# Delta-rule attention and MLP on one core: a new written-out order of the same operations

## The chip, the cores and the metric

The kernel runs on one core of a Trainium2 chip. The metric is the device time of one execution in microseconds (us), taken as the median of several runs. The engines are PE (TensorE, matrix products), DVE (VectorE), ACT (ScalarE), POOL (GpSimd) and SP (SyncE, which only issues transfers here). PEld in a profile is PE's weight loads.

## The reference

Four batches of eight heads run a recurrence over 768 tokens with a state of 48x48, and the 3072 rows of 384 that come out pass through an MLP with 2048 hidden units. Inputs and output are float32.

```python
def _attn_ref(q, k, v, beta):              # q, k, v: (4, 8, 768, 48)
    k_n = k / (np.linalg.norm(k, axis=-1, keepdims=True) + 1e-06)
    state = np.zeros((B, H, D, D), dtype=np.float32)
    for t in range(S):
        kt, vt, bt = (k_n[:, :, t].copy(), v[:, :, t].copy(), beta[:, :, t, None].copy())
        y[:, :, t] = np.einsum('bhd,bhde->bhe', q[:, :, t], state)
        v_old = np.einsum('bhde,bhd->bhe', state, kt)
        state = state + bt[:, :, :, None] * np.einsum('bhd,bhe->bhde', kt, vt - v_old)
    return y

def _moe_ref(x, w_in, w_out):              # x: (3072, 384), w_in: (384, 2048), w_out: (2048, 384)
    h = x @ w_in
    c = np.float32(np.sqrt(2.0 / np.pi))
    g = 0.5 * h * (1.0 + np.tanh(c * (h + 0.044715 * h * h * h)))
    return g @ w_out
```

## The kernel before

The tokens are cut into 12 chunks of 64. A chunk has two units (unit u belongs to chunk u // 2); a unit holds two of the four batches, one in each half of the 128 partitions, with eight heads along the free dimension. Data is bfloat16 on chip, products sum in float32 in PSUM, which has 8 banks.

The functions `load`, `norms`, `prep`, `chain` and `mlp` don't issue anything: each registers named operations with `A(engines, name, function, ...)`, together with what they read, write, allocate in PSUM and free. A name has the operation and, after the dot, its chunk or unit.

- `load(c)`: transfers of k, q and v in pieces (k3.10, q2.1, v5.01) into three raw buffers of each, taken in turn. `weights()` has four transfers from GpSimd's queue: w1.0 and w1.1 (halves of the first matrix), w2.0 and w2.1 (halves of the second). down00 to down11 read w2.0.
- `norms(c)`: sq, sum, pow, eps, nsq (or nsa on ACT), inv, ib: the norms of k and beta over their squares.
- `prep(u)`: kc, kb, qb cast and scale the tokens; T or turn (a transposing transfer) with kT turn them; GM, GQ, G2 and G form products of keys and queries (L528); ln, wpm, wpq and wp mask them (L532); X10 and X11 start an inverse (L562) and five steps refine it: A1 to A5 and B1 to B5 (L573, eight matmuls each) with rt1 to rt5 between them (L585). Each step's result goes from PSUM into a block-diagonal buffer, by one of three ways: bde (two copies of a half, L331), bdf (a copy of a half, then L337 over all partitions) or xi with two bdc (L331, L615). A step's J, C and rj are another way to its A and rt.
- `chain(c)`: the recurrence from chunk to chunk: vs, K (L645), R, Q, U (L668), Un, S (L680), Sn, O (L693), On, and X with xT or the transfer turnx. K, Q, S and O are 32 small matmuls each.
- `mlp(c)`: up0 to up15 (three matmuls each, L722), gelu0 to gelu3 (L726), down00 to down13 (four matmuls each, L733), Z0 and Z1 (L331) and the transfers out (L742, L745). up0 to up7 read w1.0, up8 to up15 w1.1.
- fill operations are products of zeros on PE in the first part.

What runs where and when is written out by hand in `ORDER`, one long text of some 1,700 words: a word is an operation's name, `:d`, `:a` or `:g` puts it on DVE, ACT or GpSimd in place of its first engine, `@n` gives its PSUM bank. Each engine works off its words in their order; `Flow.emit` puts the semaphore waits in front of an operation that needs what another engine or a transfer makes. So where an operation waits, all later words of its engine wait behind it. The place of a word relative to words of other engines means nothing for the time by itself.

Of the kernel before, what the change touches and what calls it, by code (L numbers as in the profile page):

```python
# [21 lines left out]
eps.0a betaN000 pad3:g k1.10 k1.01 kc.1 k2.00 nsq.0a inv.0a twob:d q0.1 k2.10 mlo1 pow.0b eps.0b:g q0.0:a nsq.0b:g sq.1:d v0.01:a betaA111
J1.1@3 ib.0a kb.0:g Tb.0@0 inv.0b ib.0b:g kb.1:g sum.1 kTc.0 fill4@1 betaA110 betaA101 pow.1 eps.1 nsq.1 k2.01 v0.11 inv.1 kTb.0 Tc.1@4
betaA100 ib.1:g Tb.1@2 kTb.1 kb.3:g GM.0@6 ln.0 ladj16 bdz0:g X11.0 kTc.1:a v0.10 qb.0:a GM.1@4 ln.1 X10.1:d fill45@2 fill16@1 kc.3 Tk.3@2
v0.00 fill42@0 two X10.0 Tq.0@1 X11.1 k2.11 pad2:g q1.0:a v1.10 wpm.0 A1.0@0 kTk.3:a GM.3@6 triln3 wpm.1 C1.1 sq.2 rj1.1 rt1.0 B1.0@0
# [24 lines left out]
turn.11 B4.7@1 G.9@4 wp.9 G2.9@6 ln.9 B4.6@0 up4.2@2 up5.2 up6.2 up7.2 bde40.6 up0.2@4 up8.2@6 up9.2 up10.2 up11.2 bde41.6 A5.6@0 bdc10.8:d  # L50
k8.01 xi4.7 bdc41.7 bdc40.7 kc.14 gelu1.2 up1.2 A5.7@1 up2.2 A2.8@2 up3.2 sum.7 rt5.6 rt5.7 B5.7@3 gelu2.2 sum.6 k8.10 X10.9 X11.9 A1.9@1
rt1.9 B5.6@0 up12.2@6 up13.2 up14.2 up15.2 B1.9@1 kc.13 gelu0.2 down00.2@4 bde51.7:d rt2.8 q6.0 kc.15 bde50.7 gelu3.2 q8.1 bde50.6:d K.3@2
R.3 bdf10.9 bdf11.9:d pow.6 bde51.6 G2.10@6 ln.10 B2.8@5 down01.2 pow.7 eps.6 U.3@2 v4.10 xi2.8:d bdc20.8:d bdc21.8 down02.2 v6.11 Q.3@0
# [8 lines left out]
On.4 kb.15:g A3.11@2 down00.3@4 A1.12@5 sq.8 B3.10@6 down12.3 v7.11 bde31.10 kb.14:g bde30.10 rt3.11 B3.11@0 bde31.11 out11.1 bde30.11
down01.3 down02.3 q10.0 sum.8 K.5@6 vs.5 rt1.12 B1.12@2 bde11.12 turnx.4 q8.0 A4.10@5 rt4.10 X11.13 A1.13@0 k9.00 rt1.13 bde10.12 down03.3
A4.11@5 rt4.11 Z0.3 B4.10@1 bdf40.10 turn.15 bdf41.10 down13.3 Z1.3 R.5 B4.11@0 bde41.11:d bde40.11 qb.19:g B1.13@2 up12.4@4 up13.4 bde11.13
A5.10@1 rt5.10 A2.12@3 up14.4 rt2.12 up8.4@6 B5.10@0 bde51.10:d pow.8 bde10.13 up15.4 gelu3.4 B2.12@1 bde21.12:d up9.4 A5.11@2 rt5.11 up10.4
up11.4 up0.4@4 B5.11@2 xi5.11:d up1.4 up2.4 bdc51.11:d bde50.10 A2.13@0 rt2.13 up3.4 bde20.12 gelu2.4 gelu0.4 A3.12@2 rt3.12 fill66@1
# [192 lines left out]
def bass_deltanet__then__act_gelu_tanh_kernel(  # L259
# [9 lines left out]
    B, H, S, D = q.shape  # L269
# [11 lines left out]
    A = F.add  # L281

    with nc.allow_non_contiguous_dma("strided loads"), nc.allow_low_precision("bf16 pipeline"):
# [185 lines left out]
        def prep(u):  # L469
# [26 lines left out]
            def kcopy(e, P, name, ys):  # L496
                return copy(e, kT[s][:, ys[0]:ys[-1] + 1, :, :].rearrange("p y g t -> p (y g t)"), P(name).bitcast(BF16)[:, 0:512 * len(ys)])
# [299 lines left out]
```

## Time and profile before

| | |
|---|---|
| median of 3 runs | 264.72 us (264.1, 264.72, 266.91) |
| the profiled execution | 265.58 us, span 263.8 us |
| instructions | 12,223 |
| PE busy | 244.8 us, 93% (5480 matmuls) |
| PEld busy | 190.2 us, 72% |
| DVE busy | 208.1 us, 79% |
| ACT busy | 186.5 us, 71% |
| POOL busy | 136.1 us, 52% |
| DMA | 31.86 MB, mean 121 GB/s |

The profile is of one execution. A row of a group gives the line, engine, operation and tile, the count, the busy time, the mean of one in ns, and the idle time of the engine before them with what ended it. "issue" stands for time in which an engine waited for nothing that the profile shows. The granted clock is the share of full speed that TensorE was given; where it is 0.50 a matmul takes twice as long. Rows of stretches give each engine's busy us with its count, then the granted clock, the DMA share and GB/s.

### The profile page before, as it was taken

The page shows a single profiled execution, that of the slowest core. Times are in us where ns is not written, and L with a number is a line of the kernel's source. Part 1 is how long each engine was busy: PE and PEld are TensorE (multiplying, and loading weights), DVE is VectorE, ACT ScalarE, POOL GpSimd, SP SyncE. Part 2 cuts the span into 40 slices and gives each one's busy share as a digit, 9 for nine tenths or more (in the row PEclk, how much of TensorE's full clock was granted, in tenths as well). Part 3 has the DMA queues.
Part 4 walks back from the last instruction along what each step waited for, and adds up shares of the span by engine and source line. Part 5 has one row for each costly group of instructions (what it writes and reads, how often), then busy time and mean ns, then how long its engine had stood idle before and what let it go on. Part 6 is the DMA issues. An engine that isn't in the chain of part 4 may idle for free.

```text
span 263.8 us, 12223 instructions
## 1 busy us (share of the span) xinstructions
PE 244.8 (93%) x5480; PEld 190.2 (72%) x5480; DVE 208.1 (79%) x355; ACT 186.5 (71%) x297; POOL 136.1 (52%) x197
## 2 busy tenths in 40 slices
PE   5697978699999999999999999998999999999994
PEld 1265657567787876887887988786968878878672
DVE  5788989668888898897898977999899989865000
ACT  0759878448788986988985887785855846776452
POOL 6379794679683888549266644684334120130000
PEclk9659999779999999999999999999999999999999
DMA  5999999969599984997936979631747824002122
GB/s 103 182 192 133 213 211 130 191 113 161 107 184 159 118 173 95 165 180 150 164 72 110 148 145 125 99 78 32 156 80 133 156 46 94 12 6 62 30 62 60
DMA packets 118356, 31.86 MB, mean 121 GB/s; under 512 B 112416, under 2 KB 117536, under 8 KB 118304
## 3 DMA queue, kind: packets, MB, share of 16 engines
q1 hardware_dynamic: 103408, 25.01, 56.4%
q0 software_dynamic: 2880, 3.15, 8.1%
q10 hardware_dynamic: 12016, 2.92, 5.8%
q8 instruction: 43, 0.70, 1.1%
q14 instruction: 9, 0.07, 0.1%
HBM read 20.64 MB, written 4.72 MB: 96 GB/s over the span
## 4 chain that ended last, share of the span: by engine, by line
PE 75%; DVE 7%; ACT 6%; DMA 4%; issue 3%; POOL 2%; SPq 1%; ACTq 0%; POOLq 0%
PE ps L733 23%; PE ps L722 20%; PE ps L573 18%; PE ps L528 4%; DMA kT<-tok 3%; PE ps L645 2%; ACT bd L331 2%; DMA qraw<-in_q_dram 2%; PE ps L668 2%; PE ps L693 2%; DVE rt L585 1%; PE ps L680 1%; PE ps L393 1%; DVE rl L585 1%; PE ps L493 1%
## 5 line engine op out<-in xcount | busy, mean ns | idle before, releaser
L331 ACT ACTIVATE bd<-ps 64x512 bf16<-64x512 f32 x133 | 76.6, 589 | 28.4 <-PE ps L573 26.5
L722 PE MATMUL ps<-xT,W 128*128 128x256 bf16 x576 | 77.1, 276 | 0.0
L733 PE MATMUL ps<-W,gT 128*128 128x384 bf16 x384 | 75.3, 329 | 0.3 <-issue 0.3
L726 ACT ACTIVATE gT<-ps 128x1024 bf16<-128x1024 f32 x48 | 48.1, 1019 | 14.5 <-PE ps L722 14.0
L722 PEld LDWEIGHTS ps<-xT,W 128*128 128x128 bf16 x576 | 51.3, 99 | 7.4 <-DVE st L687 0.2
L585 DVE TENSOR_TENSOR rt<-ps,two 128x512 bf16<-128x512 f32 x69 | 46.5, 682 | 6.0 <-PE ps L573 5.5
L562 POOL TENSOR_SCALAR_AFFINE_SELECT bd<-ln 64x512 bf16<-64x512 bf16 x44 | 29.0, 660 | 36.2 <-DVE ln L532 33.1
L733 PEld LDWEIGHTS ps<-W,gT 128*128 128x128 bf16 x384 | 32.9, 98 | 17.1 <-issue 1.0
L331 DVE CAST bd<-ps 64x512 bf16<-64x512 f32 x52 | 35.3, 684 | 6.1 <-PE ps L573 5.3
L532 DVE CAST_PREDICATED wp<-mup,ps 128x1024 bf16<-128x1024 uint16 (+1 forms) x28 | 29.7, 1063 | 2.6 <-PE ps L528 2.5
L457 POOL TENSOR_TENSOR nrm<-nrm,half 128x16 f32<-128x16 f32 x9 | 26.1, 2907 | 8.0 <-DVE nrm L455 8.0
L573 PE MATMUL ps<-rt,bd 128*128 128x64 bf16 x576 | 27.8, 193 | 1.9 <-DVE rt L585 0.8
L585 DVE TENSOR_TENSOR rl<-ps,two 128x384 bf16<-128x384 f32 (+1 forms) x48 | 22.9, 485 | 6.8 <-PE ps L573 6.3
L573 PE MATMUL ps<-wp,bd 128*128 128x64 bf16 (+1 forms) x576 | 26.7, 188 | 0.3 <-ACT bd L331 0.3
L573 PEld LDWEIGHTS ps<-rt,bd 128*128 128x128 bf16 x576 | 22.7, 98 | 5.2 <-DVE rt L585 1.5
L573 PEld LDWEIGHTS ps<-wp,bd 128*128 128x128 bf16 x576 | 23.2, 98 | 4.0 <-DVE bd L331 0.4
L615 POOL COPY bd<-xi 64x256 f32<-64x256 f32 x22 | 9.4, 429 | 30.0 <-ACT xi L331 21.1
L528 PE MATMUL ps<-kT 48*64 48x64 bf16 (+1 forms) x832 | 17.2, 213 | 3.0 <-issue 2.6
L484 POOL TENSOR_TENSOR tok<-kraw,nrm 128x384 bf16<-128x384 f32 x23 | 19.1, 836 | 1.3 <-PE ps L680 0.3
L532 DVE CAST_PREDICATED ln<-mlo,ps 128x512 bf16<-128x512 uint16 x24 | 16.4, 685 | 4.0 <-PE ps L528 3.8
L573 PE MATMUL ps<-ln,bd 128*128 128x48 bf16 (+1 forms) x384 | 18.4, 188 | 0.9 <-issue 0.6
L573 PE MATMUL ps<-rl,bd 128*128 128x64 bf16 x384 | 19.0, 193 | 0.0
(104 smaller groups left out, 327.4 us busy)
## 6 DMA issues: line engine op xcount, KB each, us to landing
vraw<-in_v_dram SPq DMA_DIRECT2D x42, 96.0 KB, 3.7
qraw<-in_q_dram SPq DMA_DIRECT2D x20, 192.0 KB, 4.8
kraw<-in_k_dram SPq DMA_DIRECT2D x39, 96.0 KB, 3.7
out_dram<-ob SPq DMA_DIRECT2D x19, 192.0 KB, 3.1
W<-in_moe_w_out_dram POOLq DMA_DIRECT2D x2, 768.0 KB, 10.4
W<-in_moe_w_in_dram POOLq DMA_DIRECT2D x2, 768.0 KB, 9.2
qraw<-in_q_dram ACTq DMA_DIRECT2D x4, 192.0 KB, 4.9
vraw<-in_v_dram ACTq DMA_DIRECT2D x6, 96.0 KB, 4.8
```

The source lines that it names most:

```text
L331: return e.activation(out, in_, ACT.Copy) if e is nc.scalar else e.tensor_copy(out, in_)
L457: if e is nc.scalar else e.tensor_tensor(nr[:, 1, hx], nr[:, 0, hx], half[:, hx], ALU.pow), reads=[nrn, "half"] + ["one", "roots"] * (c < ...
L484: A(("dve", "pool"), op("kb"), lambda e, P: e.tensor_tensor(kb, kr, nr[:, 5, hx].unsqueeze(2).to_broadcast(full), ALU.mult), reads=[f"kraw ...
L528: ins = e.matmul(o, kT[s][r, y, g, hf(a)], src)
L532: return e.copy_predicated(out.rearrange("p (x g) t -> p x g t", x=2), mask[:, 0:wd].bitcast(U16).unsqueeze(1).unsqueeze(1).to_broadcast([ ...
L562: A(("pool", "dve"), op(f"X1{a}"), lambda e, P, src=ln[m][hf(a), :, :], dst=bd[b_][hf(a), :, hf(a)], a=a: e.affine_select(out=dst, in_=src ...
L573: ins = e.matmul(P(name)[:, C * h + cs.start:C * h + cs.stop], bd[b_][:, h, :], rhs[:, h, cs], **kw)
L585: A(("dve",), op(f"rt{i}"), lambda e, P, i=i, cs=cs, cn=cn, r_=r_: e.tensor_tensor(r_[:, :, cs], P(ps(f"A{i}")).rearrange("p (h t) -> p h ...
L615: A(("pool", "dve"), op(f"bdc{i}{a}"), lambda e, P, src=xi[i_][hf(a), :, :], dst=bd[b_][hf(a), :, hf(a)]: e.tensor_copy(dst.bitcast(F32), ...
L722: ins = e.matmul(P(ph)[:, 256 * f:256 * f + 256].rearrange("p (x t) -> p x t", x=2), W1[:, j, 128 * (i + f):128 * (i + f) + 128], x_[:, :, ...
L726: A(("act",), f"gelu{i // 4}.{c}", lambda e, P, i=i, ph=ph: e.activation(g_[:, i:i + 4, :], P(ph).rearrange("p (f t) -> p f t", f=4), ACT. ...
L733: ins = e.matmul(P(po)[:, 0:DM], g_[:, f, 128 * b:128 * b + 128], W2[:, f, :], start=(f == 0), stop=(f == FC - 1))
```

## The change

Only the text `ORDER` changes, apart from three lines in `prep` that read a variable `late` which is always true, so that they register the same operations. The new text has the same operations in another order. In part of them the engine or the variant differs: many of the block-diagonal copies change between bde, bdf and xi with bdc; A2.1 and rt2.1 take the place of J2.1, C2.1 and rj2.1; more of sq, kc and X1 change between GpSimd, VectorE and ACT; ACT issues 37 transfers where it issued 27. On PE there are 5479 matmuls where there were 5480.

The lines of the diff around the later loads of weights, up to K.1 (first of before, then of after), and single lines from the later part:

```diff
-rt4.0 B3.1@2 bdf30.1 q3.0 pow.2 v1.11 bdf31.1 fill37@0 fill6@3 wpm.2 X11.3 X10.3 A1.3@0 rt1.3 B4.0@1 A4.1@5 rt4.1 q2.1 X10.2 X11.2 A1.2@4
-rt1.2 B1.3@0 B4.1@5 bde41.1:d bdf40.0 bdf41.0 A5.0@1 rt5.0 qb.3:g bde10.3 bde40.1 B1.2@2 bdf10.2 bdf11.2 pad4:g Tq.2@3 fill9@4 fill54@5
-B5.0@1 bde50.0 w1.0 wpq.1 Tq.3@4 kTq.3 A5.1@5 fill49@2 A2.2@6 k4.10 rt5.1 fill60@2 rt2.2 bde11.3 bde51.0 B5.1@4 bde50.1:d eps.2:g nsq.2:g
-inv.2 B2.2@0 triwpm5:g A2.3@1 rt2.3 R0a.0:g bde51.1 R0b.0:g U.0@4 Un.0:d bde21.2 bde20.2 v2.00 B2.3@1 bde20.3 A3.2@0 rt3.2 k3.01 kc.4:g
-O.0@4 On.0:d bde21.3 GQ.3@6 vs.1 B3.2@2 A3.3@0 rt3.3 X.0@1 xT.0:d bdf30.2 bdf31.2 B3.3@5 bde31.3:d k3.11 A4.2@4 up4.0@0 up5.0 up6.0 kTq.2
-bde30.3 qb.4:g wpq.3 ib.2:g kb.4:g A4.3@5 rt4.3 up7.0 tabG gelu1.0 bdz5:g up12.0@2 up0.0@6 up13.0 q3.1 B4.3@5 rt4.2 up14.0 B4.2@4 kb.5:g
-up15.0 bde41.3 bde41.2 turn.4 w2.0 qb.5:g kc.5:g k5.10 T.5@0 up1.0 up2.0 up3.0 sq.3:d sum.3 bde40.3:d k5.00 kT.5 qb.7:g k4.11 A5.3@5 rt5.3
-bde40.2 A5.2@4 rt5.2 G2.5@0 ln.5 gelu3.0 gelu0.0 S.0@2 Sn.0 G2.4@4 ln.4 G.5@6 G.4@0 K.1@2 k4.01 up8.0@4 up9.0 up10.0 up11.0 wp.4 qb.6:g R.1
-pow.3 eps.3:g nsa.3 inv.3 k5.01 ib.3 X11.5 down00.0@0 X10.4 X11.4 A1.4@1 down01.0 down10.0@2 rt1.4 B1.4@3 q4.0:a kc.7 v2.10:a gelu2.0
...
-U.8@4 Un.8 bde30.18:d v10.11 up7.7 gelu1.7 down10.7@2 A3.19@3 Q.8@4 out11.5 rt3.19 S.8@0 q11.1 O.8 On.8 turnx.8 Sn.8 G2.20@6 ln.20 X11.20
...
+q2.1 A3.1@1 rt3.1 GM.2@4 ln.2 X11.2 X10.2 A4.0@2 rt4.0 wpm.2 k4.00 Tq.1@0 B3.1@1 bdf30.1 v1.01 fill65@6 B1.3@7 fill4@2 B4.0@6 bde40.0:d
+A1.2@2 rt1.2 v1.11 fill27@4 bdf31.1 A4.1@1 rt4.1 bde41.0 A5.0@6 rt5.0 bde10.3:d B1.2@2 w1.0 B4.1@1 bde41.1:d bde11.3 B5.0@4 kTq.1 R0b.0:g
+bde10.2 bde40.1 A5.1@5 rt5.1 bde11.2 kc.4:g bdf50.0 bdf51.0 A2.2@2 B5.1@0 bde50.1 eps.2:g kTq.3 bde51.1 nsq.2:g inv.2 fill63@1 A2.3@3
+R0a.0:g rt2.2 B2.2@2 rt2.3 GQ.1@6 wpq.1 bde21.2 bde20.2 U.0@4 Un.0:d B2.3@1 bde21.3 bde20.3 A3.2@0 O.0@4 On.0 qb.4:g rt3.2 qb.2:g GQ.3@6
+wpq.3 Tq.2@3 A3.3@0 rt3.3 B3.2@2 bdf30.2 X.0@1 xT.0:d B3.3@5 bdf31.2 up4.0@0 kc.5:g A4.2@4 ib.2:g up0.0@6 qb.5:g bde31.3:d bde30.3 A4.3@5
+k3.11 kc.7 q5.1 up1.0 up2.0 up5.0 up6.0 up7.0 kTq.2 kb.4:g w2.0 rt4.3 tabG B4.3@5 rt4.2 B4.2@4 turn.4 up3.0 kb.5:g k5.01 k5.10 k5.00 T.5@2
+k5.11:a triwpm5:g kc.6:g gelu1.0 up12.0@0 up13.0 up14.0 up15.0 sq.3:g bdf40.3 sum.3 bde41.2:d bde40.2:d A5.2@4 q3.1 vs.1 pow.3 eps.3:g
+gelu0.0 bdz5:g kT.5 G2.5@2 ln.5 bdf41.3 A5.3@5 rt5.3 v3.10 rt5.2 k4.10 down00.0@6 gelu3.0 X11.5 nsa.3 v3.11:a X10.5:d inv.3 ib.3:g bdz4:g
+S.0@2 kb.6:g Sn.0 G.4@0 k4.01:a k4.11 G2.4@4 ln.4 B5.3@7 bde51.3 up8.0@2 up9.0 up10.0 up11.0 B5.2@5 wp.4 gelu2.0 down01.0 bde50.3 xi5.2:d
+G.5@0 wp.5 K.1@4 X11.4 X10.4 A1.4@2 kb.7:g q4.0 rt1.4 sq.4 down10.0@7 down02.0 k6.10 R.1 A1.5@1 qb.7:g turn.7 B1.4@0 bde10.4 down11.0
...
+Un.4:d pow.8 eps.8:g q8.1 G.12@2 G2.13@6 ln.13 v7.01:a bde21.11 down12.3 Q.4@0 wp.12 v7.00 v5.01:a bde20.11 kc.14:g q10.1:a nsq.8:g S.4@6
+O.4 On.4 Sn.4 A3.11@4 rt3.11 down00.3@2 B3.10@3 bde31.10 X11.13 X10.13 kc.15:g vs.5 A1.12@6 rt1.12 G.13@0 wp.13 B3.11@4 down01.3 bde30.11:d
...
+S.8@0 Sn.8 gelu1.7 kb.22:g O.8 G2.20@2 ln.20 X11.20 On.8 turnx.8 down00.7@5 A4.18@0 G.20@6 G2.21@2 ln.21 rt4.18 B3.19@1 bde30.19 down01.7
...
+U.10@2 down02.9 rt3.23 B3.23@0 Q.10@6 Un.10 S.10@2 O.10 bdf41.22:d A5.22@1 down13.9 bde31.23:d bde30.23 A4.23@0 Sn.10 out00.8 On.10 X.10@2
...
-                A(PE, op("T"), lambda e, P: trans(e, P, ps("T"), (0, 1, 2)), ... alt=(op("t"), 0))
+                late = True
+                A(PE, op("T"), lambda e, P: trans(e, P, ps("T"), (0, 1, 2)), ... alt=(op("t"), 0) if late else None)
...
```

Counted in matmuls of PE's queue, the words stand at these places (w1 and w2 are on GpSimd's queue; the number is of the matmuls that stand before the word):

| word | before | after |
|---|---|---|
| w2.1 | 203 | 216 |
| w1.1 | 277 | 278 |
| w1.0 | 421 | 389 |
| w2.0 | 636 | 613 |
| U.0 | 467 | 462 |
| up4.0 | 585 | 576 |
| S.0 | 689 | 692 |
| down00.0 | 813 | 688 |
| K.1 | 769 | 804 |

More of the change, by code (lines that the diff above doesn't have):

```diff
@@ L22 @@
[L22 to L25, printed above, removed]
@@ L50 @@
[L50 to L53, printed above, removed]
@@ L62 @@
[L62 to L65, printed above, removed]
@@ L78 @@
-down00.5@5 bde11.16 bde10.16:d A2.16@0 rt1.17 B1.17@7 k10.00 kc.21:d gelu0.6 k11.01:a bdf30.15:d sq.10:g vs.7 bdf40.14 bdf41.14 down13.5
-A5.14@1 bdf31.15:d sum.10 k11.11 bdf10.17 bdf11.17 v8.11 down01.5 A4.15@4 rt2.16 B2.16@0 rt5.14 B5.14@1 Z1.5 rt4.15 bde21.16 turn.18 q10.1
-qb.21:g down02.5 bde50.14:d G2.18@6 ln.18 K.7@2 R.7 B4.15@4 down03.5 bde51.14 A2.17@1 rt2.17 Z0.5:d bde20.16 A3.16@0 G.18@2 rt3.16 up8.6@6
-bde40.15 bde41.15 A5.15@1 rt5.15 B2.17@4 up9.6 up10.6 up11.6 kc.19:g turn.19 wp.18 B3.16@5 B5.15@0 v9.10 down00.6@1 bde51.15:d sq.11:g kc.22
@@ new lines @@
+eps.0b ib.0a:g kb.0 Tb.0@0 betaA111 kc.1:d q0.1 q0.0:a sq.1:d nsa.0b inv.0b sum.1 kTc.0 betaA100 pad4:g v0.00:a ladj16 ib.0b:g kb.1:g pow.1
+eps.1:g nsq.1:g fill64@3 kTb.0 betaA110 inv.1 betaA101 ib.1:g kb.3:g k2.11 two:d v0.01 Tc.1@4 fill45@5 Tb.1@1 kTc.1:a kTb.1 v1.10 GM.0@6
+ln.0 X10.0 v0.11 k3.00 q2.0:a kc.3 GM.1@4 ln.1 X10.1:d J1.1@3 k2.01 Tk.3@2 J2.0@1 X11.0 wpm.0 A1.0@0 q1.0 k2.10:a wpm.1 qb.0:a Tq.0@6
+fill56@7 X11.1 bdz2:g rt1.0 kTq.0 C1.1 rj1.1:d k3.10:a B1.0@0 kTk.3:a GM.3@6 GQ.0@4 wpm.3 ln.3 k3.01:a B1.1@3 bdf10.1:d bdf11.1:d k2.00
@@ new lines @@
+A2.16@0 up7.6 turn.18 A5.14@1 rt5.14 B1.17@2 down00.5@3 qb.21:a gelu1.6 down01.5 kb.19:g rt2.16 kc.20:g v8.00 B5.14@1 B2.16@0 bdf10.17
+bdf11.17 bdf20.16 sq.10:g sum.10 bdf50.14:d bdf51.14 K.7@4 R.7 bdf21.16 v9.10:a G2.18@6 ln.18 B4.15@2 bde40.15 down02.5 down03.5 A2.17@1
+rt2.17 A3.16@0 up8.6@6 G.18@4 bde41.15 B2.17@1 bde21.17 up9.6 A5.15@2 rt3.16 Z0.5:d bde20.17 B3.16@0 up10.6 up11.6 gelu2.6 rt5.15 B5.15@2
+bde50.15:d bde51.15 A3.17@1 down00.6@3 down01.6 down02.6 vs.8 wp.18 k11.10 sq.11:g rt3.17 kc.19:g pow.10 eps.10:g nsa.10 bdf30.16 bdf31.16
```

142 lines of the change are left out of this document (73 added, 69 removed).

## The prediction

> **What bounds the kernel now.** I read the page first, then busy time by stretches, the chain of waits around 34 to 52 us, and last single lines. The page says that TensorE (PE) is the fullest engine and where it isn't full:
>
> ```profile
> span 263.8 us, 12223 instructions
> PE 244.8 (93%) x5480; PEld 190.2 (72%) x5480; DVE 208.1 (79%) x355; ACT 186.5 (71%) x297; POOL 136.1 (52%) x197
> ...
> PE   5697978699999999999999999998999999999994
> ...
> PEclk9659999779999999999999999999999999999999
> ...
> q8 instruction: 43, 0.70, 1.1%
> ```
>
> The slices below 9 all lie in the first quarter, and there alone the granted clock falls. The next view cuts the span at the places where PE stands still (columns: busy us and count of each engine, granted clock, DMA share, GB/s):
>
> ```profile
> 0.00:28.50 28.50, 21.14 (x346) 12.72 (x347) 22.16 (x58) 16.16 (x32) 18.59 (x43) 0.82 1.00 157
> 0.00:35.42 35.42, 27.38 (x472) 17.23 (x473) 28.81 (x71) 22.90 (x45) 25.14 (x54) 0.86 1.04 167
> 35.42:41.64 6.22, 4.47 (x128) 3.69 (x127) 5.39 (x9) 4.48 (x8) 5.13 (x9) 1.00 1.08 175
> 41.64:47.82 6.18, 5.44 (x126) 4.90 (x126) 5.71 (x10) 5.46 (x9) 3.31 (x3) 1.00 1.38 163
> 47.82:50.17 2.35, 0.00 (x0) 0.00 (x0) 0.32 (x1) 1.38 (x3) 1.46 (x3) 0.86 1.02 182
> 50.17:56.32 6.15, 6.15 (x102) 4.52 (x102) 3.43 (x6) 1.75 (x2) 4.52 (x8) 0.50 0.63 107
> 60.00:260.50 200.50, 197.69 (x4602) 157.20 (x4598) 160.84 (x258) 148.34 (x230) 94.12 (x122) 1.00 0.62 108
> ```
>
> From 60 to 260.5 us PE is busy 197.69 of 200.50 us at full clock; VectorE (160.84), ScalarE (148.34) and GpSimd (94.12) have room. So the end is the moment when PE has got through its early work, plus a fixed rest. Before that the chain of waits shows:
>
> ```profile
> 35.18 0.24 PE ps L668 x5
> 35.42 0.77 issue
> 36.19 0.45 PE ps L668 x11
> ...
> 41.51 0.12 PE ps L573 x5
> 41.64 0.60 issue
> 42.24 0.25 PE ps L573 x3
> ...
> 47.59 0.22 PE ps L528 x4
> 47.82 2.35 issue
> 50.17 1.22 PE ps L528 x39
> ```
>
> Three times PE stops in the middle of one operation, waiting for nothing that the profile shows, and the stops stand at matmuls 472, 600 and 726: 128 and 126 apart. The page has 10,960 PE instructions (5480 and 5480) and 43 instruction packets: 255 instructions, or 127 matmuls with their weight loads, for each. So I read the stops as PE at the end of one block of instructions with the next not yet landed. Resume to resume they are 6.05 us (36.19 to 42.24) and 7.93 us (42.24 to 50.17) apart, so a block asked for when the one before it was entered takes that long here. What else was in flight:
>
> ```profile
> 30.62 0.78 POOL L440 DMA_DIRECT2D W<-in_moe_w_in_dram  x1
> ...
> 31.91 0.61 POOL L379 COPY wp<-tmpl 128x512 f32<-128x512 f32 x1
> ...
> 34.52 1.47 POOL L655 TENSOR_TENSOR vraw<-vraw,nrm 128x768 f32<-128x768 f32 x1
> ...
> 36.70 0.83 POOL L484 TENSOR_TENSOR tok<-kraw,nrm 128x384 bf16<-128x384 f32 x1
> 37.46 0.53 POOL L388 MEMSET bd<- 128x512 f32 x1
> ...
> 38.72 0.95 POOL L442 DMA_DIRECT2D W<-in_moe_w_out_dram  x1
> ...
> DMA to landing us min/median/max: 8.9/8.9/8.9
> DMA to landing us min/median/max: 11.7/11.7/11.7
> ```
>
> The last two lines are for the loads at 30.62 (w1.0) and 38.72 (w2.0). The second lands at 50.4, 0.3 us after PE resumes. The block waits as long as these weights do.
>
> The stop costs more than itself. In 50.17 to 56.32 the clock is 0.50, so the 6.15 us do the work of 3.08. Stop and clock: 2.35 + 3.08 = 5.43 us.
>
> **The change, part by part.** All operations stay; words move, some change engine, some change variant. I take the terms against the profiled execution's own 265.58 us (span 263.8, 1.8 around it); it is 0.86 above the median of 264.72 and inside the spread of the runs, 264.10 to 266.91. A measurement of this kernel can tell about 1% from no change.
>
> *Engines and variants.* The groups of instructions by shape (busy us, mean ns of one), and one DMA issue on ACT's queue:
>
> ```profile
> L331 ACT ACTIVATE bd<-ps 64x512 bf16<-64x512 f32 x133 | 76.6, 589 | 28.4 <-PE ps L573 26.5
> L562 POOL TENSOR_SCALAR_AFFINE_SELECT bd<-ln 64x512 bf16<-64x512 bf16 x44 | 29.0, 660 | 36.2 <-DVE ln L532 33.1
> L337 ACT ACTIVATE bd<-ps,up 128x512 bf16<-128x512 f32 x23 | 15.4, 674 | 0.9 <-DVE bd L331 0.9
> L331 POOL CAST tok<-kraw 128x384 bf16<-128x384 f32 x12 | 6.0, 503 | 0.3
> ...
> 10.26 0.61 ACTq L422 DMA_DIRECT2D qraw<-in_q_dram  x1
> ```
>
> Counted over the two orders, ACT has 14 fewer bde copies (0.589) and 17 more of the bdf kind, whose upper half is L337 (0.674); 4 fewer xi and 6 fewer kc copies; and 10 more DMA issues (0.61). GpSimd has four more sq (about 1.47 each, by the vraw row of the same size) and six more kc (0.503), against four fewer diagonal adds (0.660). Each engine's sum moves by less than 4 us, against 40, 52 and 106 us of room in 60 to 260.5. Cover: PE's own queue. Cost 0; if the cover fails where one of these stands on the recurrence from chunk to chunk, 0.1 to 0.6 us a time. A2.1 with rt2.1 for J2.1, C2.1 and rj2.1 saves one matmul: 0.
>
> *Startup.* Table load and k's first loads come earlier, and kb.0 goes to VectorE; counted along the queues this brings the first products of the chain about 2 us forward. But VectorE then has sq.1, sum.1 and kc.1 ahead of kTb.0, and kTk.2, rj1.1, bdf10.1, bdf11.1, bde40.0 and bde10.3 as further work before U.0; with 22.16 of 28.50 us busy it is the fullest there, and six operations of 0.6 us take back what was won. I take 0 at matmul 346 (bounds -1.5 and +1), and the next blocks follow at the pace of their landing, whatever the engines do.
>
> *w2.0 and the block behind it.* Between w1.0 (30.62) and w2.0 GpSimd loses vs.1 (1.47), one bdz (0.53), one kb (0.83) and a template copy (0.61), and gains qb.2, qb.5 and kc.5 at 0.5 each: 1.9 us less, so w2.0 goes out at about 36.8; ib.2 and kb.4 stay ahead of it, and ib.2 must wait for the reciprocal as before. With 8.9 to 11.7 us to landing it lands at 45.7 to 48.5. The block for matmul 726 is asked for at 42.2 again. It came with the weights before, so now at 45.7 to 48.5. PE would be there at 47.8, as now. But down00.0, the first to read these weights, now stands at matmul 688 instead of 813, ahead of S.0, G.4 and K.1 in PE's queue. In the rows:
>
> ```profile
> 46.89 0.32 PE L528 MATMUL ps<-kT 48*64 48x64 bf16 x16
> 47.04 0.42 PE L680 MATMUL ps<-us,tok 64*64 64x48 bf16 x32
> ```
>
> PE is at S.0 at 47.0. So it waits there for 0 to 1.5 us, middle 0.5, and needs 0.65 + 0.3 for down00.0 and S.0: matmul 726 at about 48.3 instead of 50.17, a gain of 1.9 (bounds: 0 if it lands as late as now, 2.35 if nothing waits).
>
> *Clock.* With waits under 1.5 us instead of 2.35, I take the half clock to be gone: -3.1 (bounds 0 and -3.1). The trace has it at 0.50 for 6.82 us, from the last part of the long stop:
>
> ```profile
> 46.08:49.50 3.42, 1.60 (x73) 1.33 (x71) 2.06 (x4) 2.68 (x5) 3.18 (x3) 1.00 1.23 199
> 49.50:56.32 6.82, 6.15 (x102) 4.52 (x102) 3.43 (x6) 2.19 (x3) 4.53 (x9) 0.50 0.64 111
> ```
>
> The Trainium skill, TensorE: Matmul & The Clock Gate, Part 1, says that the gate looks at a free-running window of about 3.4 us; the trace agrees, two windows of 3.41. By that rule the same stop costs 3.1 us in one execution and nothing in another, and the sum against the median would lose part of this term: up to 3.1 less gain.
>
> *Blocks in the dense part.* A block full of small matmuls is used up before the next lands:
>
> ```profile
> 177.10:180.05 2.95, 2.95 (x151) 2.10 (x139) 2.79 (x5) 1.99 (x4) 2.39 (x3) 1.00 0.33 72
> 180.05:180.76 0.71, 0.00 (x1) 0.00 (x0) 0.68 (x2) 0.00 (x0) 0.00 (x0) 1.00 0.01 2
> ```
>
> Counting both orders in portions of 127 from matmul 473, the new one packs Q.10, S.10, O.10 and A5.22 into one portion (96 matmuls of 64 rows or fewer), shortens the portion from S.8 by half a microsecond and that from Q.4 to S.4 by 0.8; one early portion grows. Priced at the 0.71 of the row: +0.9 (bounds 0 and +2.5).
>
> *Hand-offs in the dense part.* All are drawn anew. PE is idle 2.8 of 200.5 us there, so no more than that can be won; what can be lost has no row. I take 0 (bounds -2 and +5).
>
> Sum: 265.58 - 1.9 - 3.1 + 0.9 = 261.5 us.
>
> **The rivals.** *The block is late again (no change).* The portion before 726 ran with DMA share 1.38, loads of k and v among it, and the new order issues q5.1, k5.01, k5.11 and v3.11 there too. If the landing follows all traffic and not the weights alone, PE stops as long and the clock drops: 265.58 + 0.9 = 266.5. Against it: resume and landing of w2.0 fell together within 0.3 us. The Trainium skill, Runtime: NRT & Kernel Launch, Instruction fetch mechanics, goes further: crossing a block is mostly hidden, and the stop would then be something else that the order need not touch; the counts above speak against that.
>
> *The weights' wait takes its place (slower).* If w2.0 goes out no earlier than 38.7 (it decides from about 37.5 on, where its landing passes 49), down00.0 waits until 50.4 with everything behind it, S.0 and with it the state chain included. Then matmul 726 comes at 51.4, 1.2 later than now, the clock drops as now, S.0 is 4 us late and with the blocks' 0.9 and about 1 us of that delay coming through: 268.7.
>
> *Hand-offs worsen (slower).* The dense part loses 5 us more than the forecast has: 266.5; with half the clock loss back, 268.
>
> *Both tighten.* The two shorter stops, 0.77 and 0.60, and 2 of the 2.8 us of dense idle go as well: 261.5 - 3.4 = 258.1.
>
> *It doesn't do what it says.* The waits of VectorE for GpSimd lie where PE is full, so taking them away alone changes nothing; that is inside the forecast.
>
> **How the numbers follow.** Forecast 0.45, with its own range 259.2 to 263.6; block late again 0.20; weights' wait 0.13; hand-offs 0.12; both tighten 0.10. One per cent of 264.72 is 2.65: faster is below 262.07, slower above 267.37. Faster: 0.32 of the forecast and 0.10 of the last: 0.42. Slower: 0.13 + 0.10 and 0.05 of the late block: 0.28. Same: 0.13 of the forecast, 0.15 of the late block and 0.02 of the hand-offs: 0.30. The range from 258.0 to 268.4 leaves out the lower part of the last case and the upper parts of the two slower ones, about 0.15 to 0.2.
>
> **What would show it.** Right: the stop near matmul 726 under 1 us or in front of down00.0 (L733), the clock at 1.00 from 47 to 57, w2.0 issued by 37, matmul 726 by 48.5, and 60 to 260 as dense as now with stops of 0.5 to 1 us near matmuls 2498, 4271 and 5157. Wrong: a stop over 2 us with the clock at 0.50 behind it, w2.0 after 38, or PE under 195 us busy in 200 of the dense part.

## The result, and the profile after

The new order took 267.35 us (median of 4 runs, 266.70 to 267.62) against 264.41 us for the order before (4 runs, 261.17 to 266.91): a ratio of 1.0149, with an interval of 1.0104 to 1.0195. It is slower by 1.5 per cent, where 261.5 us and faster was forecast. Run again beside other experiments it came to 1.0136 (1.0054 to 1.0218). Medians below hold every run, ratios leave out those over 1.5 per cent above the kernel's fastest; the profiled executions of before, after_f18, astart_bdense, after_m18_w2x and before_w2early were such runs, late by their starts, so that a time of one of these starts (the 58.69 us of before, too) stands for that execution alone.

The page of the new order (profiled execution: 266.70 us) answers to the lines of before:

```profile
span 264.9 us, 12204 instructions
PE 244.2 (92%) x5472; PEld 191.1 (72%) x5479; DVE 209.0 (79%) x350; ACT 184.7 (70%) x295; POOL 136.3 (51%) x199
...
PE   7687679699999998998999989998999999999994
...
PEclk9797999899999999999999999999999999999999
```

TensorE is as full as before and its clock is better (0.981 over the span against 0.968), yet the span is 1.1 us longer. The same cut by stretches, at the places where PE stands still and at matmul 856 (857 of before), where both orders start the same kind of dense work (columns: busy us and count of each engine, granted clock, DMA share, GB/s):

```profile
0.00:35.97 35.97, 26.14 (x458) 17.49 (x462) 30.24 (x75) 20.71 (x42) 21.42 (x51) 0.91 1.01 165
35.97:47.71 11.74, 11.05 (x262) 9.25 (x262) 10.60 (x17) 10.73 (x17) 10.56 (x13) 1.00 1.35 174
47.71:50.00 2.29, 0.00 (x0) 0.00 (x1) 0.67 (x3) 0.81 (x1) 1.93 (x5) 1.00 0.92 115
50.00:57.03 7.03, 6.83 (x132) 5.13 (x133) 4.28 (x6) 2.93 (x4) 5.48 (x9) 0.76 1.22 170
57.03:261.17 204.14, 199.84 (x4624) 159.25 (x4626) 163.23 (x253) 148.99 (x231) 96.94 (x125) 1.00 0.65 108
```

The kernel before, over its last 4623 matmuls too (both rows go from the start of the first to the start of the last one):

```profile
58.69:260.07 201.38, 198.67 (x4628) 158.25 (x4625) 162.03 (x260) 149.29 (x231) 95.13 (x122) 1.00 0.63 109
```

Two things are to be seen. A stop of 2.29 us stands where the old one of 2.35 stood, so the start gains only 57.03 against 58.69 in these two executions. And the dense part takes 204.14 us in place of 201.38. The books close: 265.58 - 1.66 + 2.76 is the 266.7 of this execution, with nothing left for the tail.

The chain of waits says what the stop is:

```profile
37.48 12.41 DMA kT<-tok
49.89 0.31 issue
50.20 0.67 PE ps L529 x29
...
101.55 0.83 issue
121.98 0.84 issue
153.82 0.69 issue
181.55 0.68 issue
```

What ended last is no longer a block of instructions. G.4 (matmul 724) waits for the transposition turn.4, kT<-tok, which took 12.41 us. The last four lines are stops in the dense part, at matmuls 1990, 2498, 3257 and 3895 as PE's records count them. These records lack 7 of 5479 matmuls; counted by weight loads, which are complete, the stops stand at 1996, 2504, 3264 and 3902: whole multiples of some 127 behind 473, so ends of blocks, 3.03 us together. At each of the four, a packet of the instruction queue (q8) ended 1.2 to 1.4 us before PE went on; over the stops of this kind in all runs it is 1.2 to 1.7 us. The old order's stops there were at 1107, 3264, 3900 and 4281, 1.63 us.

The block for matmul 726 was not far behind as a limit. In 46 to 48 us the trace has one instruction packet, and none in 48 to 50:

```profile
q8 instruction: 1, 0.02, 4.7%
```

It ran from 46.25 to 47.77, so by the 1.2 to 1.7 us of the other stops (an estimate) the block alone would have held PE until 49.0 to 49.5; the transposition held it until 50.0.

The two transfers in the view of DMA issues, of after and then of before (KB each, us from issue to landing):

```profile
W<-in_moe_w_out_dram POOLq DMA_DIRECT2D x1, 768.0 KB, 8.7
...
kT<-tok SPq DMA_TRANSPOSE x1, 12.4
```

```profile
W<-in_moe_w_out_dram POOLq DMA_DIRECT2D x1, 768.0 KB, 11.7
...
kT<-tok SPq DMA_TRANSPOSE x1, 9.9
```

They have swapped their times: the weights gained 3.0 us, the transposition lost 2.5.

### The profile page after: what moved, and what is told of

The parts are those of the page before. It is cut to its first block, busy times and chain, and to the rows that moved or that the text cites. A ratio compares the mean times of both kernels' runs of the same rounds, so it can differ in the third digit from the quotient of the medians.

```text
span 264.9 us, 12204 instructions
## 1 busy us (share of the span) xinstructions
PE 244.2 (92%) x5472; PEld 191.1 (72%) x5479; DVE 209.0 (79%) x350; ACT 184.7 (70%) x295; POOL 136.3 (51%) x199
## 4 chain that ended last, share of the span: by engine, by line
PE 79%; DMA 8%; DVE 6%; issue 2%; ACTq 2%; SPq 1%; ACT 1%; POOL 1%; POOLq 0%
PE ps L734 23%; PE ps L723 23%; PE ps L574 19%; DMA kT<-tok 5%; PE ps L529 4%; PE ps L646 3%; PE ps L669 2%; DMA braw<-in_beta_dram 2%; SPq L431 1%; DVE rt L586 1%; DMA kraw<-in_k_dram 1%; PE ps L694 1%; PE ps L393 1%; PE ps L681 1%; ACTq L431 1%
## 5 line engine op out<-in xcount | busy, mean ns | idle before, releaser
L734 PE MATMUL ps<-W,gT 128*128 128x384 bf16 x384 | 73.6, 326 | 0.9 <-issue 0.8
L727 ACT ACTIVATE gT<-ps 128x1024 bf16<-128x1024 f32 x48 | 48.5, 1019 | 14.5 <-PE ps L723 14.1
L331 DVE CAST bd<-ps 64x512 bf16<-64x512 f32 x50 | 34.2, 685 | 8.8 <-PE ps L574 7.7
L563 POOL TENSOR_SCALAR_AFFINE_SELECT bd<-ln 64x512 bf16<-64x512 bf16 x40 | 26.4, 660 | 22.2 <-DVE ln L533 18.8
L574 PE MATMUL ps<-wp,bd 128*128 128x64 bf16 (+1 forms) x576 | 27.3, 189 | 2.7 <-ACT bd L331 1.2
L574 PE MATMUL ps<-rt,bd 128*128 128x64 bf16 x576 | 29.0, 195 | 0.8 <-DVE rt L586 0.4
L574 PEld LDWEIGHTS ps<-rt,bd 128*128 128x128 bf16 x576 | 23.7, 99 | 5.1 <-DVE rt L586 1.4
L616 POOL COPY bd<-xi 64x256 f32<-64x256 f32 x19 | 7.6, 401 | 38.4 <-DVE xi L331 22.0
L484 POOL TENSOR_TENSOR tok<-kraw,nrm 128x384 bf16<-128x384 f32 x21 | 17.6, 844 | 5.4 <-PE ps L681 4.9
L574 PEld LDWEIGHTS ps<-ln,bd 128*128 128x128 bf16 x384 | 15.5, 97 | 6.0 <-DVE bd L337 1.9
```

The source lines that it names most:

```text
L331: return e.activation(out, in_, ACT.Copy) if e is nc.scalar else e.tensor_copy(out, in_)
L484: A(("dve", "pool"), op("kb"), lambda e, P: e.tensor_tensor(kb, kr, nr[:, 5, hx].unsqueeze(2).to_broadcast(full), ALU.mult), reads=[f"kraw ...
L563: A(("pool", "dve"), op(f"X1{a}"), lambda e, P, src=ln[m][hf(a), :, :], dst=bd[b_][hf(a), :, hf(a)], a=a: e.affine_select(out=dst, in_=src ...
L574: ins = e.matmul(P(name)[:, C * h + cs.start:C * h + cs.stop], bd[b_][:, h, :], rhs[:, h, cs], **kw)
L727: A(("act",), f"gelu{i // 4}.{c}", lambda e, P, i=i, ph=ph: e.activation(g_[:, i:i + 4, :], P(ph).rearrange("p (f t) -> p f t", f=4), ACT. ...
L734: ins = e.matmul(P(po)[:, 0:DM], g_[:, f, 128 * b:128 * b + 128], W2[:, f, :], start=(f == 0), stop=(f == FC - 1))
```

## The experiments

Two theories stood against each other. The first: the dense part is slower because other work now lies at the ends of its instruction blocks. The second: the start lost it, by the transposition that waits beside the weights. A third was that the old order has better hand-offs, whatever the blocks do.

### 18 fills left out, in the new order and in the old

Fills are matmuls on zeros in the first part. 18 fewer of them move every later block end 18 matmuls on in the work; no other word changes.

```diff
 after_m18 (new order), before_m18 (old order)
-fill64 fill45 fill56 fill36 fill9 fill65 fill4 fill27 fill63 fill54 fill41 fill52 fill20 fill23 fill42 fill25 fill49 fill12
-fill45 fill16 fill42 fill36 fill1 fill41 fill27 fill37 fill6 fill9 fill54 fill49 fill60 fill4 fill25 fill28 fill46 fill23
```

> The new order with 18 fill matmuls of the first 10 us and of the waits up to 35 us left out, nothing else changed; every block of instructions then ends 18 matmuls later in the work. Theory (the stops in the dense part are ends of instruction blocks full of small matmuls): of the stops near matmuls 1990, 2498, 3257 and 3895, 3.0 us in all, at least three vanish, together under 1 us is left, and the median falls by 2.0 to 2.5 us to about 265. Rival (they are waits of the operations themselves, which the profile can't name): the same operations stop as long as before, and the time stays within 0.7 us of the new order's.

> The old order with 18 fill matmuls left out in the same way. Theory of the blocks: its stops near 1107, 3258, 3891 and 4281 (1.6 us) fall under 0.6 us, and the median falls by 1.0 to 1.6 us; in the startup the block ends move too, so the stop of 2.35 us near 726 stands 18 matmuls later in the work, at K.1 or G.5. Rival: the stops stay with their operations (G2.7, O.6, K.8, down02.7), time within 0.7 us of the old order's.

Measured: 263.89 us for the new order with 18 fewer (ratio 1.0003, 0.9958 to 1.0048), 263.02 for the old (0.9951, 0.9900 to 1.0001). The new order's dense part:

```profile
55.56:255.76 200.20, 198.87 (x4628) 159.16 (x4625) 162.69 (x253) 149.26 (x232) 98.20 (x126) 1.00 0.67 111
```

200.20 us against 204.14 for the same operations in the same order, with stops of 0.18 us left (at matmul 2504 of its stream). The old order's goes from 201.38 only to 201.44: its stops didn't fall under 0.6 us as expected but stand elsewhere, 1.7 us in all, 1.2 of it at matmul 1867. So the dense part's loss goes when its blocks end elsewhere. What the start contributes is not told apart yet: the fills left out sit there.

### The transposition replaced, and the weights early in the old order

```diff
 after_t4: the k of chunk 4 transposed by TensorE and ScalarE, 12 fills less for the 12 matmuls more
-turn.4
+T.4@2 kT.4:a
-fill64 fill45 fill56 fill36 fill9 fill65 fill4 fill27 fill63 fill54 fill41 fill52
 before_w2early (old order): w2.0 ahead of turn.4
-bdz5:g ... kb.5:g ... turn.4 w2.0
+w2.0 bdz5:g ... kb.5:g ... turn.4
```

> The new order with unit 4's turning done by PE and ACT (T.4, kT.4) in place of the transposing transfer turn.4, and 12 fills left out so that the blocks end where they did. Theory 1 (the transfers of the first 50 us share one capacity, and something lands late whatever comes first): the stop ahead of G.4 goes, and PE stops at the end of the block near 726 until about 48.5 to 49.2, so the median falls by 0.5 to 1.5 us. Rival (the transposing transfer alone held PE): PE passes matmul 726 by 47.7, the clock stays at 1.00, and the median falls by 3 to 4 us.

> The old order with one word moved: w2.0 issued ahead of bdz5 and kb.5, about 1.4 us earlier, as in the new order. Theory 1 (one capacity): the block for matmul 726 lands earlier, with the weights, near 48, but turn.4, until now landed at 47.4, lands near 49.5 to 50, G2.4 waits for it, matmul 726 comes at 49.5 to 50.3 and the median stays within 1.0 us of the old order's. Rival (the step of the prediction): turn.4 as before, matmul 726 near 48.3, the clock at 1.00, median 2 to 4 us lower.

Measured: 268.01 us (1.0148, 1.0060 to 1.0236) and 263.91 us (1.0031, 0.9977 to 1.0085). Without turn.4 the wait at G.4 is gone, but my edit made another: T.5 waits 1.2 us, from 45.5 us on, for ScalarE's copy of kT.4, and G.4 starts at 50.79, no sooner. Its dense part kept the loss (205.2 us, 4.4 us of stops). The run says nothing against the second theory and nothing for it. In the old order w2.0 and turn.4, issued 0.1 us apart, landed at 52.89 and 50.70, and G2.4 (matmul 721) waited for the transposition as G.4 did in the new one; the time hardly moved.

### One order's start with the other's dense part

```diff
 astart_bdense: the new words up to matmul 897, then the old ones; fill0 fill2 fill3 added in the start (5480 matmuls)
 bstart_adense: the old words up to matmul 897, then the new ones; matmuls padded to 5479
```

> The new order's words up to TensorE's matmul 897, then the old order's, with early fills added until the number of matmuls is the old one, so that the blocks of the dense part end at the same operations as in the old order. Theory (the time was lost in the dense part: 204.6 us from matmul 850 to the last one against 201.6 in the old order): the dense part takes 201 to 202 us again, with stops near matmuls 3264, 3900 and 4281 only, and the time is that of the kernel before or up to 1.5 us less (about 262 to 263.5). Rival (the new start lost it, by the wait for the transposition at matmul 724): it stays near 267.

> The reverse: the old order's words up to TensorE's matmul 897, then the new order's, matmuls padded to the new number. Theory (dense part): 204 to 205.5 us from matmul 850 on, with stops near 1990, 2498, 3257 and 3895, and a time 2.5 to 4 us over the kernel before (266 to 267). Rival (start): about 263, as before.

Measured: 267.18 us (1.0136, 1.0059 to 1.0213) and 268.37 us (1.0167, 1.0079 to 1.0256). Both are slow, and as a test of the time this failed: at the seam PE waits 2.5 us (matmuls 915 to 1063) in the one and 2.1 us (922 to 978) in the other, for copies that the joined orders bring late. From A4.6 (matmul 1588 or 1597) to the last matmul, well behind the seam, the parts keep their kind: 172.3 us with the old words (172.4 in the kernel before), 174.2 with the new ones (175.9 after, 174.2 when it ran again).

### Other fills left out

```diff
 after_f18 (new order), before_f18 (old order)
-fill1 fill14 fill16 fill60 fill46 fill6 fill37 fill26 fill28 fill47 fill49 fill12 fill65 fill4 fill27 fill63 fill64 fill45
-fill14 fill12 fill56 fill65 fill63 fill22 fill52 fill26 fill64 fill20 fill23 fill46 fill28 fill25 fill4 fill45 fill16 fill42
```

> The new order with 18 fills left out, other ones than in the run that left out 18 spread over the start: here the first 12, which run before any data is there, and 6 later ones; those at matmuls 24 to 30, 135, 224 and 269 stay. The blocks of the dense part end at the same operations as with the other 18. Theory (where blocks end decides): the dense part again takes 200.5 to 201.5 us with under 0.5 us of stops, and the time is 262 to 264 us, less than the new order's 267.3 by 3 to 5. Rival (the gain came from the start, by which fills are there): the dense part stays at 204 to 205 us and the time over 265.

> The old order with its first 15 fills and 3 more left out, in place of 18 spread ones. Theory (blocks): the dense part takes 200 to 201.7 us, as with the other 18 (201.6), against 201.6 in the old order, and the time is 261.5 to 263.5. If the fills kept here hold the granted clock up between 20 and 36 us, U.0 starts at 35 to 36 us and the time is at the lower end; rival (the early fills are what warms the clock): U.0 after 36.5 us and 263.5 to 266.

Measured: 267.89 us as a median of 12 widely spread runs (263.18 to 274.81; ratio 1.0066, 1.0007 to 1.0125), and 262.61 (0.9978, 0.9937 to 1.0019), with U.0 at 36.4 us, between the two forecasts. The dense part of the new order, once more with 18 fewer:

```profile
64.67:265.72 201.05, 198.99 (x4628) 159.16 (x4625) 162.79 (x253) 148.74 (x231) 97.12 (x125) 1.00 0.61 110
```

201.05 us, as expected, with 1.0 us of stops in place of under 0.5, though other fills were left out. The time was not as expected: in the profiled execution w2.0 took 15.18 us to land, turn.4 beside it 13.01, and PE stood 7.0 us at down00.0. It is the longest wait of the second theory's kind in these profiles.

### The weights moved

```diff
 after_m18_w2x: as after_m18, and w2.0 behind w1.0
-kTq.2 kb.4:g w2.0 rt4.3
+R0b.0:g ... w2.0 kc.4:g
 before_f18_w2x: as before_f18, and w2.0 behind w1.0
-turn.4 w2.0 qb.5:g
+w2.0 triwpm5:g
 after_w2late: the new order, w2.0 behind turn.4
-kb.4:g w2.0 rt4.3 ... turn.4 up3.0 kb.5:g k5.01 k5.10
+kb.4:g rt4.3 ... turn.4 up3.0 kb.5:g k5.01 w2.0 k5.10
```

> The new order with the 18 spread fills left out, and the weights' DMA w2.0 moved to just behind w1.0 and R0b.0 on GpSimd's queue (issue near 32 us in place of 37). Theory (the transposition of turn.4 is late because w2.0 is issued with it: 10.9 to 12.4 us in three runs of that kind, against 5.9 to 9.9 in three where it went 1.2 us ahead): turn.4 lands in 6 to 9 us, by 43 to 46; G.4 doesn't wait; what is left near matmul 720 is the block's stop of up to 1.4 us; the time is 0.5 to 2 us under the run with the 18 left out alone (261.5 to 263.5 where that was 263.9). Rival (the transposition is slow for other reasons): it lands in 10 to 12 us all the same and the time stays at 264. A loss is possible where w1.0 lands later and up4.0 waits for it: then 265.

> The old order with its first 15 fills and 3 more left out, and w2.0 moved to just behind w1.0 on GpSimd's queue (issue near 32 us in place of 39.8). By the theory of a shared capacity, turn.4 and the instruction block for matmul 726 land earlier: the block by 48 in place of 49.2, the stop at 726 falls from 1.3 to under 0.5 us, and the time is 0.5 to 1 us under that kernel without the move (262.6), 0.8 per cent under the kernel before. Rival: up4.0 waits for w1.0 and the gain is gone (262.6 or over).

> The new order with nothing left out and w2.0 moved behind turn.4, kb.5 and k5.01, so that the transposition is issued over 1 us ahead of the weights, as in the old order. Theory (one capacity, two transfers): turn.4 lands 2 to 4 us sooner (by 46 to 48), w2.0 later (47.5 to 50), and TensorE now waits at down00.0 (matmul 688) for the weights, 1 to 3 us; the time stays within 1.5 us of the new order's 267.3. The dense part keeps its 204 to 205 us from matmul 850 on. Rival (putting w2.0 early was what cost the time): 263 to 264.

Measured: 265.02 us (0.9996, 0.9948 to 1.0045), 262.74 us (0.9961, 0.9930 to 0.9992) and 271.52 us (median of 4, 267.32 to 271.88). In the first the transposition landed in 5.50 us, as the theory wants, but w2.0 took 13.37 and the time stayed. In the second turn.4 took 10.04, against the theory; the stop at 726 went, but PE waited 2.1 us at matmul 639 for a copy of VectorE. The third didn't do what I meant: GpSimd reached w2.0 at 38.35 and SP reached turn.4 only at 38.83, so they went together again; they landed at 49.42 and 51.18, and PE waited 0.8 us for the one and 0.6 for the other. before_f18_w2x is the one version here with an interval below 1: 0.4 per cent under the kernel before.

### Block ends shifted behind the start

These leave the start as it is and put tiny matmuls (32 columns) behind it.

```diff
 after_d8, after_d54, after_d108 (new order); before_d46 (old order, in front of B5.2)
-A1.5@1
+fill70 ... fill77 (or fill123, fill177) A1.5@1
-e.matmul(P(n), wz[:, 0:128], wz[:, :])
+e.matmul(P(n)[:, 0:w], wz[:, 0:128], wz[:, 0:w])      # w = 512 if i < 70 else 32
```

> The new order with nothing left out or moved, and 8 tiny fills (32 columns wide, 0.06 us or less each, under 0.5 us in all) added in front of A1.5 at matmul 852, behind the start. They move the ends of all later blocks 8 matmuls ahead in the work and nothing else. Theory (where a block ends decides): the stops in the dense part grow from 3.0 us to 4.5 to 6, the part from matmul 850 on from 204.6 to 206.5 to 208, and the time to 269 to 270.5. Rival (the dense part is slower by its hand-offs, whichever block an operation falls in): 0.3 to 0.5 us more than the new order, 267.8.

> The same with 54 tiny fills (2.5 to 4.5 us by themselves): the block ends move to where short stretches of work fill whole blocks. Theory: the stops of the dense part rise from 3.0 to 3.7 us to 7 to 9 us, the part behind the fills takes 208 to 212 us, and the time is 274 to 280. Rival: 204 to 206 us and 270 to 272.

> The new order with 108 tiny fills (32 columns) in front of A1.5 at matmul 852, behind the start. A block holds 126.6 matmuls, so 108 more put the block ends of the dense part where 18 fewer put them. The fills themselves cost 5 to 9 us (8 of them cost 0.3 to 0.7). Theory (where a block ends decides): the part from the first matmul behind the fills to the last one takes 200.5 to 202.5 us with under 1 us of stops, 3 to 4 us less than in the new order (204.6), although nothing of the start or of the later order has changed. Rival (the fills left out in the start did it by warming the clock or by the times of transfers): that part stays at 204 to 206 us with 3 to 4 us of stops. The time itself says less: 269 to 273 by the first, 273 to 277 by the second.

> The old order with 46 tiny fills (2 to 4 us by themselves) in front of B5.2 at matmul 853. Theory (the old order is no better in itself, its blocks end at better places): stops rise from 1.6 to 6 to 8 us, the part behind the fills takes 206 to 210 us against 201.6, and the time is 270 to 275. Rival (the old order has better hand-offs, whatever the blocks do): the part stays at 201 to 203 us and the time at 266 to 268.

> The new order itself beside these: 266.5 to 268, with 204.5 to 205.7 us from matmul 850 on and 3 to 4.4 us of stops there.

Measured: 269.71, 272.57, 271.82, 268.58 and 266.01 us; ratios 1.0221 (1.0167 to 1.0275), 1.0387 (1.0314 to 1.0461), 1.0378 (1.0293 to 1.0463), 1.0251 (1.0181 to 1.0322) and 1.0136. The fills, with the waits in front of them, took 1.19, 1.69, 3.77 and 1.16 us. What counts are the same 4623 matmuls behind them. With 54, with 108, the old order with 46, and the new order untouched:

```profile
58.61:266.77 208.16, 200.51 (x4628) 160.54 (x4625) 161.88 (x251) 149.12 (x231) 96.79 (x124) 0.99 0.62 105
```

```profile
62.45:265.49 203.04, 199.42 (x4627) 159.62 (x4625) 162.13 (x251) 148.85 (x231) 96.74 (x124) 1.00 0.64 107
```

```profile
57.21:263.00 205.79, 199.09 (x4628) 158.17 (x4625) 163.99 (x258) 149.06 (x230) 94.81 (x122) 1.00 0.61 106
```

```profile
58.00:260.59 202.59, 199.19 (x4627) 159.29 (x4625) 163.30 (x253) 149.00 (x232) 97.03 (x125) 1.00 0.64 109
```

The stops of the 54 in its chain of waits:

```profile
64.61 2.17 issue
...
88.51 1.25 issue
...
124.92 2.01 issue
...
162.28 0.84 issue
...
186.52 0.51 issue
```

They stand at matmuls 1107, 1616, 2505, 3392 and 3902 of the stream. The old order's blocks end at 1107 and 3900 too, the new one's at 2504 and 3902 (by weight loads): the same counts, whatever operation lies there. In one table, stops being those that wait for nothing the profile shows:

| kernel | stops in the dense part, us | dense part, us |
|---|---|---|
| new order, + 54 | 6.9 | 208.2 |
| new order, + 8 (1.4 us more at block ends stand beside a ScalarE copy) | 2.7 | 204.7 |
| new order (after, after_w2late, after_t4, after_again) | 3.0, 3.2, 4.4, 2.3 | 204.1, 204.6, 205.2, 202.6 |
| new order, + 108 | 1.5 | 203.0 |
| new order, - 18 (m18, f18, m18_w2x) | 0.2, 1.0, 1.8 | 200.2, 201.1, 201.8 |
| old order, + 46 | 4.7 | 205.8 |
| old order (before, before_w2early) | 1.6, 1.9 | 201.4, 202.0 |
| old order, - 18 (m18, f18, f18_w2x) | 1.7, 1.2, 0.4 | 201.4, 200.9, 200.1 |

Where a block ends moves the dense part of the new order by up to 8.0 us and that of the old one by up to 5.7, with the order unchanged: the first theory is shown. Not all of the 8.0 is stops: with the 54, the clock is 0.50 for 3.4 us behind the first stop (67.9 to 71.3 us), which costs some 1.7 us. The direction came as expected with 54, 108 and 46 more, the sizes mostly did not. 8 more gave 204.7 and not 206.5; the longer time of that run is not of the dense part: in its profile the start took 58.5 us and the fills 1.2. 108 more gave 203.0, above the 200.5 to 202.5 expected; the copies behind the fills wait too (0.9 us), so that 108 more are not wholly 18 fewer. 54 more gave 272.57 us where 274 or more was expected, and 46 more in the old order 268.58 us with 4.7 us of stops where 270 and 6 or more were. The new order itself came out faster than expected, 202.6 us in the dense part and not 204.5. And the stops don't carry all of it: without them the new order needs 200.0 to 202.0 us, the old one 199.7 to 201.1. Some 0.8 us are left to hand-offs (or to what a stop costs behind itself); that split wasn't settled.

### The two transfers, over all runs

| issue | turn.4, us to landing | w2.0, us to landing |
|---|---|---|
| together, w2.0 up to 0.5 us ahead (after, after_again, + 8, + 54, + 108, m18, w2late, f18, astart_bdense, before_w2early) | 12.4, 12.3, 11.4, 12.4, 11.8, 10.9, 12.4, 13.0, 11.8, 10.0 | 8.7, 11.3, 14.6, 9.0, 14.7, 9.6, 11.1, 15.2, 9.3, 12.3 |
| w2.0 6.6 and 10.9 us ahead (before_f18_w2x, after_m18_w2x) | 10.0, 5.5 | 12.5, 13.4 |
| turn.4 1.2 us ahead (before, before_m18, before_f18, before_d46, bstart_adense) | 9.9, 7.8, 5.9, 8.2, 11.7 | 11.7, 10.2, 9.6, 10.4, 9.4 |

In the five new starts that nothing was changed in, PE waits 2.3, 2.8, 2.5, 1.4 and 2.6 us for the later of the two, now at G.4 and now at down00.0. When it ran again, the chain showed:

```profile
37.79 11.25 DMA W<-in_moe_w_out_dram
49.04 0.05 issue
49.09 1.46 PE ps L734 x4
```

These five starts reach matmul 852 to 856 at 56.8 to 58.6 us; the old order's two that nothing was changed in (before, before_d46) at 58.7 and 56.0. So few profiles show no gain of the one start over the other.

## Why the prediction was wrong, step by step

**w2.0 and the block behind it: the step that failed.** The weights went out at 37.40 (forecast 36.8) and landed at 46.06, inside 45.7 to 48.5. But matmul 726 came at 50.2 and not at 48.3 (48.45 by the step's own terms, 47.0 + 0.5 + 0.65 + 0.3): the step let only the weights and the block be late. It said what is queued at down00.0 and S.0, and not that G.4, right behind S.0, needs turn.4. That transposition was issued at 37.55 and took 9.9 us in the profile I had, so it landed at 47.45, 0.1 us ahead of G2.4, which read it first (47.59). It had no slack, and the weights were moved in front of it. The step's other premise, that the block lands with the weights, failed too. The block's packet ended 1.7 us before the weights landed in before (48.72 and 50.44) and in before_f18 (47.68 and 49.40), but 1.7 us after them in after (47.77 and 46.06) and 2.4 us after them in after_m18 (48.98 and 46.59). So with turn.4 in time, by the 49.0 to 49.5 above, about half of the 1.9 would still have been missing (an estimate). The rival "the weights' wait takes its place" had the right kind of event with the wrong condition: down00.0 waits with w2.0 issued at 37.2 to 37.8 too. The gain of 1.9 is 0.

**Clock.** Half of it held in the profiled execution: 57.03 against 58.69 is a gain of 1.66, about what one window of half clock less gives. Cut in steps of 2 us the half clock lasts about 3.4 us (50.4 to 53.9) against 6.82 before; when the new order ran again it lasted 6.8. By the Trainium skill, TensorE: Matmul & The Clock Gate, Part 1, the gate works in windows of about 3.4 us; the traces agree, with one window and two. The rows of after, then those of its second run:

```profile
48.00:50.00 2.00, 0.00 (x0) 0.00 (x1) 0.58 (x2) 0.81 (x1) 1.73 (x4) 1.00 1.05 131
50.00:52.00 2.00, 1.80 (x44) 1.64 (x45) 1.09 (x2) 0.55 (x1) 0.84 (x2) 0.61 1.46 186
52.00:54.00 2.00, 2.00 (x17) 1.45 (x15) 0.73 (x1) 0.04 (x1) 1.86 (x4) 0.53 1.47 189
54.00:56.00 2.00, 2.00 (x71) 1.39 (x68) 1.43 (x2) 1.50 (x2) 1.75 (x5) 1.00 0.81 121
```

```profile
48.00:50.00 2.00, 0.91 (x3) 0.43 (x4) 0.05 (x1) 0.00 (x0) 1.10 (x3) 0.52 1.13 160
50.00:52.00 2.00, 2.00 (x72) 1.46 (x71) 0.19 (x1) 0.81 (x1) 0.80 (x1) 0.50 1.37 188
52.00:54.00 2.00, 2.00 (x15) 1.47 (x13) 1.63 (x2) 0.59 (x1) 1.24 (x3) 0.50 1.48 160
54.00:56.00 2.00, 2.00 (x36) 1.35 (x36) 0.69 (x1) 1.10 (x2) 1.80 (x4) 0.78 1.46 156
```

So a stop at this place was followed by one window (2.29 us in after, 2.93 in bstart_adense), by two (2.35 in before, 2.78 in after_again) or by none (2.50 in after_d8 and 2.64 in after_d108, with clock 1.00 from 46 to 60 us; 1.35 in before_f18); the kernel before has executions at a mean clock of 0.999 and 260.6 us beside the profiled one at 0.968 and 265.58. So this term was a property of one execution, not of the order: 3.1 was taken off a number that the median (264.41) holds only in part.

**Blocks in the dense part.** The mechanism was right, the size short: the stops went from 1.63 to 3.03 us, 1.4 more where 0.9 was priced, and 0.6 more when the new order ran again (2.3). Of the places named (2498, 4271, 5157) the first came (2504 by weight loads), with 1996, 3264 and 3902 beside it. The Trainium skill, Runtime: NRT & Kernel Launch, Instruction fetch mechanics, has the crossing of a block as mostly hidden; these runs differ, with up to 2.17 us at one crossing and 6.9 us in all.

**Hand-offs.** The forecast took them as 0 with +5 as a bound. The dense part lost 2.76 us and the stops explain 1.40 of it; of the other 1.36, PE's busy time has 1.17 (199.84 against 198.67). Why PE's busy time grew stays open; with 18 fills fewer it was 198.87 in the same order.

**Engines and variants.** No engine but PE fills the dense part in either order, and none of their sums decides the time; this held. U.0 began at 35.97, 0.8 later than before, inside the bounds of the startup term.

**The sum as it came.** From 265.58: start -1.7 (forecast -5.0), dense part +2.8 (forecast +0.9). By the medians the start gave nothing: of the 2.9 us between 264.41 and 267.35 the dense part's 2.8 is nearly all, and when the order ran again (262.23 to 266.01, dense part 1.2 longer) the start even lost some 2.6, by difference. How much of the loss is the start's is thus not fixed by these runs. The range of 258.0 to 268.4 holds 267.35, but none of the cases behind it had the wait for turn.4; the likeliest case was the wrong one.

## What to carry to other kernels

Where PE is full and its instructions come in blocks, count the blocks: 18 matmuls fewer in the start made the rest of the new order 1 to 5 us shorter and that of the old one 0 to 2, so compare two orders only with the block ends in mind. Before a transfer is moved forward, list every other one in flight with its landing and its reader, above all the one that lands just in time. Take a stop's price from the median and not from one execution, when the clock behind the stop differs from run to run.

## What the runs showed of the hardware that was not expected

The transposition kT<-tok, which took 3.6 to 7.2 us at other places and 5.5 with the weights issued 10.9 us ahead (turn.4 in after_m18_w2x), took 10.0 to 13.0 us when issued together with 768 KB of weights, and these took anything from 8.7 to 15.2 us in the same place. And a stop at the end of a block cost about its own length in the dense part: over the new order's runs from 0.2 to 6.9 us of stops the stretch grew from 200.2 to 208.2, with 1.7 us of it by the half clock of the one run.
